# Linear attention and a gated two-layer network on one core: batch 0 loaded by casting transfers, more seven-product groups, chunk 4's sums by accumulating transfers, and normalising shared between VectorE, ScalarE and GpSimd

## The chip, the cores and the metric

The kernel runs on one core of one Trainium2 chip. The time is that of one execution on the device, in microseconds. Three runs of the kernel before took 278.95, 280.96 and 282.47 us; the median, 280.96, is what a changed kernel is compared with. One more execution was profiled: it took 283.07 us, of which the span from the first to the last instruction is 281.3 us.

## What is computed

```python
# q, k, v: (8, 8, 576, 64) float32;  theta = pi/2 * position/576
phi(x) = concat(relu(x)*cos(theta), relu(x)*sin(theta))     # 64 -> 128 features
kv  = einsum('bhsf,bhsd->bhfd', phi(k), v)
z   = sum over s of phi(k)
att = einsum('bhsf,bhfd->bhsd', phi(q), kv) / (einsum('bhsf,bhf->bhs', phi(q), z) + 1e-6)
x   = att, heads side by side: (4608, 512)
h   = x @ w_in                                              # (512, 2048)
out = (h * cos(h)) @ w_out                                  # (2048, 512), float32
```

The matrix products run in float16 with float32 sums.

## The kernel before

**Chunks.** Eight batches of 576 tokens are computed as nine chunks of 512 tokens: chunks 0 to 7 hold four tiles of 128 tokens of their batch (NT = 4), and chunk 8 holds the 64 tokens that each batch has left (R = 64, two batches to a tile). A batch lies on the partitions so that one tile index t is one column of `RAW`; tile 4 is the half-filled one, and its empty half is set to zero by a memset of `raw[nm][:, :, NT, :]`.

**Attention of a batch.** `load` (L264) brings q, k and v. For batches 1 to 7 these are transfers from POOL's queue that cast float32 to float16 on the way into `RAW`. Batch 0 is loaded by SP's queue as float32 into the buffers `raw0`, which borrow `gT` and `TT` (L206). `prep` (L282, L295 on ACT and L296 on DVE) applies relu and the cosine or sine of one tile and writes `KQ` (`kp` for k, `qp` for q). `cast_v` (L307, L308) copies v beside a column of ones into `V1`. `kv` (L319) sums the products over tiles in PSUM; the ones give z as the 65th column; `kvz` is its float16 copy. q is transposed by `q_pe` (L348 on PE, copies L352, L354) for batches 0 and 1 and by DMA (`q_dma`, L358) for the others. `num` (L380) multiplies the transposed q with kvz into a pair of PSUM banks; then `norm` takes the 65th columns plus 1e-6 (`den`, L412), the reciprocal (`rec`, L414) and the scaled rows (`x16`, L405), one DVE step of three instructions. `x_pe` (L437, copy L441) or `x_dma` (L447) transposes x16 into `xT`.

**Layers.** Layer 1 of chunks 0 and 1 runs as matmuls of 256 columns (L493); from chunk 2 on as plain matmuls of 512 columns (L525) or as groups of seven products (L620). Such a group replaces the 16 plain matmuls of four column blocks of w_in by 28 of 256 columns, after sums of w_in (`w_in_sums`, L556) and of xT (L577), and puts the products together again: three copies on ACT (L628), three sums on DVE (L632), one double cosine and product (L643, L649). `gate` (L467 on ACT, L469 on DVE) forms h*cos(h). `FAST` says how many of a chunk's groups run that way, the others being plain:

```python
todo = [g for g in range(NJT // 4) if g >= nf]
for g in range(NJT // 4):
    if g < nf:
        layer1_fast(c, g, X, xk)
    if g < len(todo):
        for j in [2 * todo[g] + i + JH * hf for i in range(2) for hf in range(2)]:
            layer1_plain(c, j, X, xk)
```

NJT is 16. Layer 2 of chunk 0 is plain (L722); from chunk 1 on it is seven products too (L796) over sums of g (L773, L826 on DVE). For the chunks in `ACC` two of these sums are accumulating transfers from POOL's queue (`add_dma`, L755).

**Order.** Every step is added to a list with its engine, the time that it is booked with, what it reads and what it writes. The text `ORDER` then says, as differences, in which order the steps are issued, and with a letter on which engine a step with a choice runs (D, A, P). The booked times and due times had a part in making that text and have none when the kernel is built. So each engine's instructions stand in one fixed order, and a step that waits holds up everything behind it on its engine. POOL's queue issues loads, w_in and w_out (L881, L887), the accumulating transfers and the stores of finished rows (L683).

**Start.** `warm` (L870) issues matmuls of 128x512 on a constant tile WZ (a part of S2, set by POOL's memset): 14 at the front, 16 ahead of kv, and 4, 3 and 2 between the first tiles (`FILL`). `weights` (L873) holds w_in's loads back until k of batch 0 has landed, by a copy of four elements.

Of the kernel before, what the change touches and what calls it, by code (L numbers as in the profile page):

```python
# [10 lines left out]
AF = mybir.ActivationFunctionType  # L11
ALU = mybir.AluOpType
# [4 lines left out]
ACC = (5, 6, 7)  # L17
POW = False
FAST = ((3, 2), (4, 2), (5, 2), (6, 4), (7, 4), (8, 4))
ORDER = (  # L20
    "1 6 1 -3 4 -6 7 1 1 1 1 1 18 1 -5 -7 -1 14 -5 -4 107D 1A -109 6 -25 17 -19 33 1D 8A 92 -136 "
    "38A 4D 93 -92D -3A 5D -31 27A -2D -24 22D 10A 3A -1D -3D 2A -23 -9 37D 2A -1D 2 -4A -1D 86 "
    "-115 35 1 -32 -9 42 -29 30 -26 27 77 -75 -1 -44 49 -1 3 -1 72 -76 9 -8 7 3 -1 67 -71 8 -7 8 "
    "1 59 -63 7 -6 65 9D -18 -49 63D 1D -67 62 -57 -4 3 71D -12 -55 -2 62D -61 4 -2 1 4 -2 57D "
    "-56 4 -2 58D -57 4 -2 54D -53 4 -2 50D -49 4 -2 50D -49 4 -2 175 -122D -4A -48 4 171 -173 "
    "63D -58 -2 -2 3 2 2 43A 4D -48 4 -2 38D -33 -4 2 55D -54 4 -2 53A -2D -50 36 -34 54 -14A 13D "
    "-52 4 47D -1D -21 6D 123 -104 -24 4 6D -3 18 -12D -2 -3 117 -93 -20 15 4 -5 101 -112 13 23 "
    "75 -110 17 -47 51 -1 -7 24 -68 45 8 14 710 -721 13 -8 90D -89 716 -721 -3 -5 100D -79 -20 8 "
    "86A 2A 2D 4D -93 88A -84 26 64A -81 73D -85 267 -272 95D 4D 117 -207 91D -69 -21 207 -182 "
    "82D -15 -70 188 -183 -19 15 75A 113 -120 -65 2 2 681 -617A -65 4 -2 73D -72 4 -2 66D -5A -60 "  # L30
    "4 -2 59 -27 24 -51 -36 91D -86 32 -5 61 -59 30 144A -205 32 60A 118A -175 58 1A -32 -26 61A "
    "-1 -54 -41 202A -4 -196 34 2 60 112A -11 -162 62 1 -61 -32 94 106A 6A -151 43 -1 -2 103A "
    "-200 101 -64 61 -63 172A -102 -104 38 159D -160 4 -2 311 -145A -165 63 -2 -59 2 158D -97 95A "
    "-153 55 244 -303 2 63 1 -3 4 -62 -51 119 101A -100 -4 232 -238 4 238 -299 62 -66 3 159 -157 "
    "161D 3A -67 -96 159A -209 140 78A -7 -99 31 -2 6 65D -95 27 -2 72 2A -68 59 12D -101 90 148D "
    "-136 135D -134A -76 4 -36 104 -62 -5 72A 135D -132 -73 -1 5 67 123 12D -134 -71 4 1 187 5A "
    "-196 10 -48 110 -230 163 2 190A -349 158 67 2 -64 -44 -2 230A -121 -61 63 -68 197A -235 42 "
    "65 -68 69 1 -65 5 61 119A -183 4 -5 66 117A -116 1 -115 53 -4 67 122A -184 69 109A -172 57 "
    "-67 5 314 -250 -118 117 -62 -53 239A 130 -252 -59 2 305 -123A -121 -67 7 309 -311 178 -182 7 "
    "-186 364A -238 54 187A -91 6 -4 2 88 -249 241 -79 91A -73 66 -82 -158 161 -40 38 4 -46 128D "  # L40
    "-83 -160 150 12 -4 5 -11 21 -8 -45 55 200A -133A -68 -172 375A -131D -245 2 244 2A -85 208A "
    "-188 -18 -159 237 -9 -231 163 2 -48 -115 2 240A -78 81 -83 84 113 -239 59 -176 -4 122 126 "
    "-77 203A -256 241 -187 -55 134 -245 363A -119 -65 188A -197 -10 -47 133 112A 149 -332 -61 53 "
    "9 71 -248 119 1 49 71 -59 68 -131 132 111A -240 49 8 66 -60 174D -107 -69 -59 60 196A -13D "
    "-114 2 -75 74 -60 -71 133 -83 -48 70 -9 71 -70 -61 1 61 193A -7D -185 -61 254 -21D -165 168A "
    "-173 -17 -44 60 315 -313 11 175A 126 -311 190A -186 -68 255A -184 87 -89 91 88A -86 -92 173 "
    "-168 171D -174 175 -83 -88 87 -157 67 185A -8 -85 -163 255A -98 7 76 -113 127 -75 63 -114 38 "
    "91 -252 162 216A -382 169 -5 -159 253 -91 90 -251 173 -50 130 -91 -161 123 256A -206 201A "
    "-223 -156 259 -90 -1 20 186 -204 90 -71 -59 131 -90 -172 180 202A -255 246 -110 2 -70 189A "
    "-210 200 -201 23 68 -5 -73 -11 -45 69 67 -134 49 197A -202 91 2 -1 -133 47 5 199D 1A -251 "  # L50
    "134 -79 -58 250A -112 -88 9 196A -250 50 -4 -50 63 76 -75 74 -133 238A 2D -179 -63 64 335 "
    "-351 8 12 69 -134 1 396 -142A -253 60 338 -334 186D -184 -5 -9 347 -334 4 -2 -5 200A -15 13A "
    "-188 91 -93 -2 183A -176 184D -188 181 -85 -91 89 83 -247 167 -95 96 92 -97 99D -90 235A "
    "-238 -163 247A -180 100 1 80 1D -254 75 99 -5 -37 45 -46 116 -241 398A -226 85 138A -226 -5 "
    "-169 254A -79 -169 257 -262 254 -72 -175 256 -130 50 -6 -176 183 -48 26 230 -261 6 256 -128 "
    "-131 -2 -130 177 -44 131 -88 2 5 213A -204 -13 5 -46 127 -72 -54 260A -214 83 -128 127 -69 "
    "197D -126 -75 5 -13 219A -210 75 1 1 -85 -51 66 -2 -4 213D -147 -121 132 -72 214A -226 214D "
    "-137 150A -228 16 190A -191 -59 130 -84 15 213A -207 -20 15 52 146D -196 -11 -52 256A 16 "
    "-210 2 -67 277D -199 -77 67 2 -66 68 196A -12D -177 -4 -4 198 -196 -78 269 7A 7 -268 270A "
    "-206 2 94 -90 190A -98 -6 -161 72 94 101 -105 98 -92 18 75 -130 42 -41 52 -10 -168 179 -22 "  # L60
    "-30 44 10 91 -421 420 -113 7 108 -87 -20 18 -183 168 3 96A -266 273 1 -106 -41 56 92 -114 12 "
    "12 -192 181 -12 114 -105 15 -192 283 1 -103 -47 144 -276 191 10 -68 -134 284 -84 73 -80 8 -4 "
    "-66 75 79 -87 -63 68 83 -109 -38 69 -14 13 -71 63 10 78 -102 -47 83 -84 82 -24 -9 -46 148 "
    "-68 -10 -69 1 69 -7 85 -67 69 -75 -20 16 5 10 -82 68 15 -23 20 -7 -75 83 -3 6 94 -179 180 "
    "-93 -1 -16 76 39 -105 103 -95 3 93 -182 69 21 -88 -1 86 -84 88 88 23 -18 16 -20 7 14 -113 "
    "101 17 -199 196 -15 -42 44 -182 199 -203 181 23 -61 46 16 -61 43 -182 201 -18 -38 -5 45 -334 "
    "337 14 1 -14 -193 146 44 4 17 -3 6 -2 -31 35 -1 -2 -63 67 16 49 -62 -29 -44 74 13 -10 -79 3 "
    "74 -23 40 -16 12 -35 -48 88 -87 83 -235 217 7 1 -17 -203 235 -14 16 -1 39 -127 90 -14 53 "
    "-132 136 -56 14 -90 77 -76 128 -74 75 -128 129 2 -39 -91 133 -45 4 43 -1 -41 -92 69 -9 87 "
    "-12 -65 75 -9 10 -145 77 59 -49 60 3 -13 14 -150 151 -64 53 -134 135 -64 -70 84 -90 7 120 14 "  # L70
    "-140 90 60 -15 -127 143 9 -8 -310 250 69 -34 -126 156 5 -4 -155 150 -8 14 7 -159 86 74 -13 9 "
    "16 -9 -2 -77 90 -12 -74 85 -44 35 1 10 -86 -2 43 39 -78 87 -183 95 90 -32 -56 47 40 -30 -56 "
    "89 -88 72 -71 75 11 -10 -75 61 26 -16 17 -26 -60 70 -71 91 -12 -77 86 4 -88 89 -4 -86 2 75 "
    "-71 -3 4 84 -87 88 5 -89 -3 82 11 -88 90 -1 -5 -85 86 6 -8 15 -12 7 6 -7 3 5 -6 2 8 -7 8 -4 "
    "5 1 1 -6 10 -9 8 -2 1 3 1 1 1 1 1 1 "
# [53 lines left out]
def kernel(  # L129
# [44 lines left out]
    def sb(name, shape, dt=F16):  # L174
# [31 lines left out]
    home0 = {"k": gT[0].rearrange("p h t j s -> p (h t j s)"),  # L206
             "q": gT[1].rearrange("p h t j s -> p (h t j s)"),
             "v": TT.rearrange("p n j s -> p (n j s)")}
    raw0 = {nm: heads_tokens(t.bitcast(F32)[:, 0:NR]) for nm, t in home0.items()}
# [20 lines left out]
    FILL = (4, 3, 2, 0)  # L230
# [3 lines left out]
    LATE_BY, LATE_W = (0.0, 0.8, 1.5, 1.0), 0.6  # L234
    LOAD_RATE = (355.0, 360.0)
    ORDER0, ORDER1 = "qkv", "kqv"
# [4 lines left out]
    B0, B1, B2, BP = 20.0, 56.0, 80.0, 27.0  # L241
# [12 lines left out]
    def either(due, cost, fn, rd, wr):  # L254

        lat = {"DVE": 0.13, "ACT": 0.15, "POOL": 0.15}
        pl.add([(e, cost[e], cost[e] + lat[e], fn[e]) for e in cost], 0, 0, due, None, rd, wr, port=True)
# [6 lines left out]
    def load(b, nm, due, hs=(slice(0, H),)):  # L264

        m, n = (raw0 if b == 0 else raw)[nm], b % 2
        q, eng = (nc.sync, "SP") if b == 0 else (nc.gpsimd, "POOL")
        for h in hs:
            five, four = tokens(src[nm][b][h])
            part = [(nm, hh, b == 0) for hh in range(H)[h]]  # L270

            def go5(h=h, five=five):
                q.dma_start(out=blocks(m, n)[:, h], in_=five)

            def go4(h=h, four=four):
                q.dma_start(out=blocks(m, 1 - n)[:, h, 0:NT, :], in_=four)
            nb = len(part) * R * D * 4 / 1e3
            occ = 0.65 if b == 0 else 0.9
            for go, k, x in ((go4, NT, 1 - n), (go5, NT + 1, n)):
                pl.add(eng, occ, 0, due, go, (), [(y, x) for y in part], dma=(nb * k, LOAD_RATE[b > 0]),  # L280
                       lane="first" if b == 0 else None, late=LATE_BY[min(b, 3)])
# [742 lines left out]
```

## Time and profile before

| | |
|---|---|
| median of three runs | 280.96 us (278.95 to 282.47) |
| profiled execution | 283.07 us, span 281.3 us |
| granted TensorE clock, mean | 0.994 |
| busy: PE, DVE, ACT, POOL | 269.9, 251.8, 210.5, 60.3 us |
| first layer-1 matmul | 21.56 us |
| layer 1 of chunk 0 in PE's order | 21.5 to 36.3 us |
| last matmul ends | about 277 us |
| instructions | 6759 |

PE is TensorE's matmuls and PEld its weight loads; DVE is VectorE, ACT ScalarE, POOL GpSimd, SP SyncE. Busy time is the time in which at least one instruction of an engine runs; matmuls overlap each other, so 256 columns take 0.109 us one behind the other (8 in 0.87 us in the chain of work) although one of them lasts 0.273. In a table of stretches the columns are busy time by engine, the granted clock of PE as a share of full speed, the busy share of the DMA engines, and GB/s moved. In a list of waits each line gives the engine and line that waits, what it waited for, the total, the number of times and the longest.

### The profile page before, as it was taken

What the parts mean: (1) busy time and instruction counts of PE and PEld (TensorE: products, weight loads), DVE (VectorE), ACT (ScalarE), POOL (GpSimd) and SP (SyncE); (2) the same over time, 40 slices, a digit from 0 to 9 for tenths busy, and PEclk for the clock granted to TensorE, in tenths of its full rate; (3) what the DMA queues carried; (4) which work ended last, traced back from release to release, by engine and by line L of the source; (5) the groups of instructions that cost most, each with busy time, mean ns of one, the idle gap of its engine ahead of it and who ended that gap; (6) DMA issues with size and microseconds to landing.
All of it is one profiled execution on the core that took longest, in us unless ns stands there. A gap on an engine that the chain in (4) does not pass through costs nothing.

```text
span 281.3 us, 6759 instructions
## 1 busy us (share of the span) xinstructions
PE 269.9 (96%) x2691; PEld 216.4 (77%) x2691; DVE 251.8 (90%) x484; ACT 210.5 (75%) x353; POOL 60.3 (21%) x98
## 2 busy tenths in 40 slices
PE   7799999998999799999999999999999999999994
PEld 2568876865956478787878787779988888888883
DVE  2879999897999799999999999999999999988952
ACT  2856876898899969889899987987576776657420
POOL 1472141410403300502323030002110220121300
PEclk9799999999999999999999999999999999999999
DMA  6999999999999999999999999486850434075124
GB/s 208 327 201 203 201 190 177 184 147 185 125 188 156 193 226 145 193 172 156 210 199 107 179 189 161 77 166 150 192 94 2 87 107 125 3 224 114 75 77 149
DMA packets 78463, 44.06 MB, mean 157 GB/s; under 512 B 46176, under 2 KB 75360, under 8 KB 78432
## 3 DMA queue, kind: packets, MB, share of 16 engines
q0 software_dynamic: 29856, 28.12, 57.5%
q1 hardware_dynamic: 47840, 14.95, 30.9%
q10 hardware_dynamic: 736, 0.57, 0.6%
q8 instruction: 21, 0.34, 0.5%
q14 instruction: 10, 0.08, 0.1%
HBM read 36.74 MB, written 9.44 MB: 164 GB/s over the span
## 4 chain that ended last, share of the span: by engine, by line
PE 82%; DMA 9%; DVE 5%; ACT 2%; issue 1%; SPq 0%; ACTq 0%
PE M L796 33%; PE M L620 14%; PE M L525 8%; DMA qT<-KQ 7%; PE TR L620 6%; PE M L493 4%; PE M L722 4%; PE ATT L380 3%; DVE gT L469 3%; PE ATT L319 3%; DMA gT<-in_q_dram 2%; PE TR L525 2%; PE M L348 2%; PE ATT L870 1%; ACT KQ L295 1%
## 5 line engine op out<-in xcount | busy, mean ns | idle before, releaser
L796 PEld LDWEIGHTS <-gT 128*128 128x128 f16 x560 | 54.1, 98 | 7.6
L295 ACT ACTIVATE KQ<-RAW,CS 128x512 f16<-128x512 f16 x86 | 59.1, 720 | 0.0
L796 PE MATMUL M<-w_out_sb,gT 128*128 128x256 f16 x448 | 56.2, 273 | 0.0
L467 ACT ACTIVATE ch<-M 128x512 f32<-128x512 f32 x75 | 44.1, 598 | 13.2 <-PE M L493 4.4
L469 DVE TENSOR_TENSOR gT<-M,ch 128x512 f16<-128x512 f32 x73 | 49.1, 684 | 3.1 <-ACT ch L467 2.3
L525 PE MATMUL M<-xT,w_in_sb 128*128 128x512 f16 x136 | 33.1, 379 | 0.0
L796 PE MATMUL M<-TT,S 128*128 128x256 f16 x256 | 32.0, 273 | 0.0
L807 ACT ACTIVATE ost<-M 128x512 f32<-128x512 f32 x32 | 19.1, 597 | 17.2 <-PE M L796 13.4
L493 PE MATMUL M<-xT,w_in_sb 128*128 128x256 f16 x256 | 29.7, 272 | 0.0
L683 POOL DMA_DIRECT2D out_dram<-ost x32 | 18.8, 611 | 47.2 <-DVE ost L811 25.7
L620 PEld LDWEIGHTS <-w_in_sb 128*128 128x128 f16 x264 | 25.4, 98 | 3.7
L796 PEld LDWEIGHTS <-S 128*128 128x128 f16 x256 | 24.6, 98 | 3.0
L628 ACT ACTIVATE Z<-M 128x512 f32<-128x512 f32 x31 | 18.2, 600 | 11.6 <-PE M L620 8.6
L493 PEld LDWEIGHTS <-w_in_sb 128*128 128x128 f16 x256 | 24.6, 98 | 3.0
L632 DVE TENSOR_TENSOR Z<-M,Z 128x512 f32<-128x512 f32 x38 | 25.4, 683 | 1.1 <-PE M L620 0.6
L525 PEld LDWEIGHTS <-w_in_sb 128*128 128x128 f16 x160 | 14.8, 98 | 13.1
L405 DVE TENSOR_TENSOR x<-ATT,rec 128x512 f16<-128x512 f32 x32 | 22.1, 691 | 1.1
L380 PEld LDWEIGHTS <-qT 128*128 128x128 f16 x320 | 15.7, 98 | 7.3 <-DMA qT<-KQ 3.7
L811 DVE TENSOR_TENSOR ost<-M,ost 128x512 f32<-128x512 f32 x24 | 16.4, 684 | 4.2 <-PE M L796 4.0
L380 PE MATMUL ATT<-kvz,qT 128*128 128x65 f16 x288 | 16.4, 194 | 3.0 <-DMA qT<-KQ 2.6
L296 DVE TENSOR_SCALAR KQ<-RAW,CS 128x512 f16<-128x512 f16 x54 | 18.3, 350 | 0.2 <-DMA RAW<-in_k_dram 0.2
L773 DVE TENSOR_TENSOR S<-gT 128x2048 f16<-128x2048 f16 x14 | 17.0, 1217 | 0.1
(133 smaller groups left out, 482.3 us busy)
## 6 DMA issues: line engine op xcount, KB each, us to landing
out_dram<-ost POOLq DMA_DIRECT2D x32, 256.0 KB, 4.7
RAW<-in_k_dram POOLq DMA_DIRECT2D x7, 320.0 KB, 5.3
RAW<-in_q_dram POOLq DMA_DIRECT2D x7, 320.0 KB, 7.6
w_in_sb<-in_moe_w_in_dram POOLq DMA_DIRECT2D x4, 512.0 KB, 9.8
w_out_sb<-in_moe_w_out_dram POOLq DMA_DIRECT2D x4, 512.0 KB, 12.1
RAW<-in_v_dram POOLq DMA_DIRECT2D x6, 320.0 KB, 7.4
RAW<-in_k_dram POOLq DMA_DIRECT2D x7, 256.0 KB, 6.4
RAW<-in_q_dram POOLq DMA_DIRECT2D x7, 256.0 KB, 6.7
```

Source lines behind the costliest of these rows:

```text
L295: fn = {"ACT": lambda: nc.scalar.activation(out=out_, in_=in_, func=AF.Relu, scale=sc), "DVE": lambda: nc.vector.tensor_scalar(out=out_, i ...
L380: nc.tensor.matmul(bank[hb][:, hh * D1:(hh + 1) * D1], lhsT=a[:, h, :], rhs=z[:, h, :], start=(i == 0), stop=(i == len(parts) - 1))
L405: nc.vector.tensor_tensor(out=split(x16[n][:, hs, :], k), in0=A[:, :, :, 0:D], in1=split(rec[n][:, hs], k).unsqueeze(3).broadcast_to((P, k ...
L467: act(0.5, due, lambda: nc.scalar.activation(out=ch[c], in_=bank, func=AF.Sin, bias=math.pi / 2.0, scale=1.0), [key], [("ch", c)])
L469: mul(due, 0.61, lambda q: q.tensor_tensor(out=dst, in0=bank.rearrange("p (j s) -> p j s", j=2), in1=ch[c].rearrange("p (j s) -> p j s", j ...
L493: nc.tensor.matmul(M1[m][:, jj * 2 * P:(jj + 1) * 2 * P], lhsT=w_in_sb[:, cc, j * P:(j + 1) * P], rhs=X[:, cc, ts], start=(cc == 0), stop= ...
L525: nc.tensor.matmul(M, lhsT=w_in_sb[:, cc, j * P:(j + 1) * P], rhs=X[:, cc, :], start=(cc == 0), stop=(cc == NCT - 1))
L620: nc.tensor.matmul(bank[0][:, j * TH:(j + 1) * TH], lhsT=a(cc, j), rhs=b[:, cc, :], start=(first and j == 0 and cc == 0), stop=(last and j ...
L632: dve(0.61, due + 0.3, lambda: nc.vector.tensor_tensor(out=dst, in0=bank[0], in1=dst, op=ALU.add), [bank[1], key], [key])
L683: pl.add(eng, 0.9 if eng == "POOL" else 0.65, 0, due, lambda: q.dma_start(out=dst, in_=src_), keys, [], dma=(nb, 355.0))
L796: nc.tensor.matmul(bank[0][:, tt * MH:(tt + 1) * MH], lhsT=a[:, j, tt * P:(tt + 1) * P], rhs=b[:, j, :], start=(first and (apart or tt == ...
L807: act(0.5, due, lambda: nc.scalar.activation(out=dst, in_=view(bank), func=AF.Copy), [bank[1]], dk)
```

## The change

- Batch 0 is loaded like the others: casting transfers on POOL's queue into `RAW`, k first, then v by halves of the heads, q by parts (tiles 0 and 1, tiles 2 to 4). Batch 1 uses the same form, and the buffers `raw0` are gone. The memsets of the empty halves stand in `setup`, once, on DVE, as do those of WZ, of V1's ones and of MINUS.
- k and v come before q in the first attention; 19 warming matmuls at the front and no others. w_in is no longer held back, and its first quarter comes in two pieces.
- Layer 1 of chunks 0 and 1 does its first quarter in pieces of 128 columns, each waiting for its own tile of xT.
- `FAST` asks for 26 groups in all, where it asked for 18.
- `ACC` holds chunk 4 too.
- The normalising is three steps with a choice of engine: the den sums on DVE or ACT, the reciprocal on DVE or, as a power of -1, on POOL, the scaling on DVE.
- `ORDER` is another text. In it, of 36 tiles, 28 have their den sums on ACT and 16 their reciprocal on POOL; 78 preps run on DVE and 82 on ACT, where it was 66 and 94.

```diff
-ACC = (5, 6, 7)
-POW = False
-FAST = ((3, 2), (4, 2), (5, 2), (6, 4), (7, 4), (8, 4))
+ACC = (4, 5, 6, 7)
+FAST = ((3, 3), (4, 4), (5, 4), (6, 5), (7, 5), (8, 5))
 ORDER = (
...
-    raw0 = {nm: heads_tokens(t.bitcast(F32)[:, 0:NR]) for nm, t in home0.items()}
...
-    FILL = (4, 3, 2, 0)
...
-    def load(b, nm, due, hs=(slice(0, H),)):
+    def load(b, nm, due, hs=slice(0, H), ts=range(NT + 1)):
 
-        m, n = (raw0 if b == 0 else raw)[nm], b % 2
-        q, eng = (nc.sync, "SP") if b == 0 else (nc.gpsimd, "POOL")
...
+        m, n = raw[nm], b % 2
+        five, four = tokens(src[nm][b])
+        heads = range(H)[hs]
+        for ap, k, x in ((four, NT, 1 - n), (five, NT + 1, n)):
+            t = slice(ts[0], min(ts[-1] + 1, k))
+            dst, ap = blocks(m, x)[:, hs, t, :], ap[:, hs, t, :]
+            wr = [((nm, h, i), x) for h in heads for i in sorted({min(j, 2) // 2 for j in ts})]
+            pl.add("POOL", 0.72, 0, due, lambda dst=dst, ap=ap: nc.gpsimd.dma_start(out=dst, in_=ap),
+                   (), wr, dma=(len(heads) * R * D * 4 / 1e3 * (t.stop - t.start), "ld"),
+                   late=LD_LATE[min(b, 2)])
...
-        def norm():
+        def sums():
             for A, (hs, k, ks) in zip(N, cut):
                 nc.vector.tensor_scalar_add(
                     out=split(den[n][:, hs], k), in0=A[:, :, :, D], scalar1=1e-6)
-            nc.vector.reciprocal(out=rec[n], in_=den[n])
-            scaled()
...
+        m = len(cut)
+        either(due, {"DVE": 0.1 + 0.06 * m, "ACT": 0.21 * m}, {"DVE": sums, "ACT": dens}, keys, [("den", n)], False)
+        either(due, {"DVE": 0.2, "POOL": 1.75}, {"DVE": lambda: nc.vector.reciprocal(out=rec[n], in_=den[n]), "POOL": recs},
+               [("den", n)], [("rec", n)], False)
+        dve(0.62 + 0.07 * m, due, scaled, keys + [("rec", n)], [("x16", n)])
         return n
...
+                        wk = [("w_in", quarter, jp)]
+                        if quarter == 0:
+                            for i in range(2):
+                                pe(2 * NCT, MMT, due, lambda i=i, mm=mm: mm(i * P, (i + 1) * P),
+                                   [xk[2 * hf + i]] + wk + [("M1", m)] * i, [("M1", m, 1)] if i else [("M1", m)])
+                        else:
+                            pe(2 * NCT, MMH, due, lambda mm=mm: mm(0, 2 * P), xk[2 * hf:2 * hf + 2] + wk,
+                               [("M1", m), ("M1", m, 1)])
...
     def setup():
-        nc.gpsimd.memset(S2[:, 0:2, :], 0.5)
+        nc.vector.memset(S2[:, 0:2, :], 0.5)
         nc.vector.memset(PIH, math.pi / 2.0)
+        for nm in "kvq":
+            nc.vector.memset(raw[nm][:, :, NT, :], 0.0)
+        nc.vector.memset(V1[:, :, :, D], 1.0)
+        nc.vector.memset(MINUS, -1.0)
...
     def weights():
-        def hold():
...
         for g in range(4):
-            fs = slice(g * Dff // 4, (g + 1) * Dff // 4)
...
+            for e in ((0,), (1,)) if g == 0 else ((0, 1),):
+                fs = slice(g * Dff // 4 + e[0] * Dff // 8, g * Dff // 4 + (e[-1] + 1) * Dff // 8)
...
     def first_attention():
...
-        warm(14, 6.5)
...
+        warm(19, 6.1)
+        load(0, "k", 0)
+        for h in HALVES:
+            load(0, "v", 1, h)
+        load(0, "q", 2, ts=(0, 1))
         weights()
...
+        load(0, "q", 3, ts=(2, 3, 4))
...
-            if FILL[t]:
-                warm(FILL[t], 0.2157 * FILL[t], M1[1],
-                     [(("ATT", "M2")[t % 2], 1)], [("M1", 1), ("fill", t)])
-            x_pe(0, t, t, *BANKS[3 - t % 2], "ACT", 8 + t, [("fill", t)])
```

`recs` is in the kernel before too, not called there: `nc.gpsimd.tensor_tensor(out=rec[n], in0=den[n], in1=MINUS, op=ALU.pow)`. On POOL a library reload stands in the built program ahead of the first of these.

## The prediction

> **What bounds the kernel now.** I read the page's busy shares first, then the busy time by stage (the windows), then the start in order of time, then the waits of PE.
>
> ```profile
> PE 269.9 (96%) x2691; PEld 216.4 (77%) x2691; DVE 251.8 (90%) x484; ACT 210.5 (75%) x353; POOL 60.3 (21%) x98
> ```
>
> PE is never far from full; the question is where the other 4% lies and how close DVE is.
>
> ```profile
> 0.00:8.20 8.20, 5.02 (x14) 1.73 (x14) 2.19 (x6) 2.19 (x4) 0.95 (x7) 1.00 0.71 230
> 9.50:11.20 1.70, 1.70 (x17) 1.70 (x18) 1.41 (x5) 0.96 (x2) 0.35 (x1) 0.50 1.08 357
> 21.50:36.30 14.80, 14.80 (x145) 13.27 (x143) 14.06 (x34) 11.29 (x20) 3.46 (x5) 1.00 1.30 203
> 41.10:77.40 36.30, 35.51 (x371) 26.06 (x369) 32.88 (x73) 29.77 (x52) 10.01 (x15) 1.00 1.24 164
> 77.40:100.00 22.60, 20.74 (x184) 12.68 (x181) 20.02 (x43) 19.70 (x34) 5.75 (x9) 1.00 1.24 181
> 100.00:200.00 100.00, 100.00 (x1033) 80.98 (x1031) 96.98 (x182) 87.31 (x147) 18.77 (x30) 1.00 1.01 168
> 260.80:275.70 14.90, 14.90 (x139) 13.36 (x137) 10.96 (x17) 4.39 (x7) 2.12 (x4) 1.00 0.18 71
> ```
>
> (Columns: stretch, length, busy time of PE, PEld, DVE, ACT, POOL, granted clock, DMA share, GB/s.) From 21.5 us PE is full but for 3.2 us in all (0.54 between 36.3 and 41.1, 0.79, 1.86). From 100 to 200, where the changed groups lie, PE has no hole and DVE has 3%: two engines bound it together. The start is 21.5 us in which PE does almost no layer work, and its last 5.6 us of the span are the tail.
>
> ```profile
> 8.28 0.90 PE L348 MATMUL TR<-IDENT,KQ 128*128 128x128 f16 x8 [1.94 <-ACT KQ L295]
> 9.50 1.89 PE L348 MATMUL M<-IDENT,KQ 128*128 128x128 f16 x16 [0.33 <-ACT KQ L295]
> 11.18 3.96 PE L870 MATMUL ATT<-S 128*128 128x512 f16 x16
> 14.98 0.61 PE L348 MATMUL M<-IDENT,KQ 128*128 128x128 f16 x8
> 15.43 1.37 PE L319 MATMUL M<-V,KQ 128*128 128x65 f16 x40
> 21.56 1.04 PE L493 MATMUL M<-xT,w_in_sb 128*128 128x256 f16 x8
> ```
>
> The filler of 16 (L870) runs while v is still landing (its casts start at 13.27); from there to the first layer-1 matmul is 8.3 us of chain.
>
> ```profile
> PE ATT L380 <- DMA qT<-KQ: 2.6, 2, 1.8
> ```
>
> This is the largest hole after the start.
>
> **The change, part by part.** All against the profiled execution: 283.07 us, of which 281.3 is the span. The three runs have a median of 280.96, so I scale the ratio of the spans to that.
>
> *Start.* Batch 0's loads move from SP to POOL as casting loads into RAW. SP's first issue is at 0.73; POOL's first now waits for DVE's memset of k's tail (S, then RAW; the RAW memset is 0.27 each), so about 1.5. In before, the first casting load was issued at 10.85 and its landing took 4.7; plain loads moved 357 to 365 GB/s, casting ones 203 to 206 (written bytes, half of those read), so q, k and v take 3.54 MB/0.365 = 9.7 us or 1.77/0.2 = 8.9 us: the stream itself gains under 1 us. With first bytes 2.1 us after issue (10.85 to the fall of the rate at 13) I get k and the first q part landed at about 8.3, v at 11.3, the rest of q at 12.9, against 13.3 for v before. Ten issues of 0.7 us are done by about 8.6, within that stream.
> Work behind it: 20 preps of float32 (DVE 0.48, ACT 0.71) become float16 ones (DVE 0.35, ACT 0.72); k and v come first, q after. From v: cast 0.35 and 0.28, kv 20 matmuls twice (0.6 each), kvz on ACT 0.39, num 0.29, den 0.16, a prep, reciprocal 0.20, scaling 0.69, then qT's copy 0.68 because in PE's order tile 2's num stands ahead of x_pe; x_pe 0.39, den on ACT 0.2, xT 0.60: about 6.1 with hops, so layer 1 at 17.4 against 21.56. It then takes 8 pieces of 128 columns (0.45 each) and 12 groups at the 0.87 of PE; the 14.8 us stage before becomes about 15.7, since DVE still has six multiplies, scalings and preps to catch up on. End of layer 1 of chunk 0: 33.1, was 36.3.
> That is with a warm clock. The three small fillers and the filler of 16 are gone; 19 matmuls at the front end at about 7.4 and then PE has only two transposes until kv. The clock row above reads 0.50 in 9.5 to 11.2 after 1.9 us without work, and it was 1.00 again from 13. The idle stretch now is longer, so I take kv, num and the first pieces at half clock: 3.4 us of PE work at double length, partly beside DVE, up to 1.6 us more (34.7). Gain between 3.2 and 1.6; I take 2.3, between them, as DVE paces part of that stretch. The Trainium skill ("TensorE: Matmul & The Clock Gate", Part 1) says that the clock is halved by default and is released only after some 3.4 us of sustained work; the trace agrees with its half clock. By that rule alone the gain is the 1.6 end and the total 0.7 us later; with no gating it is the 3.2 end.
>
> *POOL's queue at the start.* w_in now stands behind 1.77 MB, k and q of batch 1 between its pieces. Added up at 0.2 MB/us from 3.6: w_in's four quarters at about 15.5, 22, 25 and 28, v of batch 1 at 31, half of w_out at 37.5. Before they were (same rate from 13.4) 19 to 30, 33 and 38. PE wants them at 17.4, 22, 25.7, 29 and 38: hidden, by under 1 us. If POOL stalls at a load that waits for a prep (RAW is now shared by batches 0 and 1, as the separate buffers are gone), all behind it is late one for one.
>
> *Groups.* L620 has 504 matmuls before and 644 in the changed order: 18 groups become 23, not 26, since the loops run over NJT // 4 = 4 groups and the three 5s act as 4. Five more (one in chunk 3, two each in 4 and 5). PE: per group 28 x 0.109 - 16 x 0.216 = -0.41, so -2.0; the 128-column pieces add 128 x 0.056 - 64 x 0.109 = +0.2. DVE per group: three sums (0.684) and a double multiply (1.217) for two fewer single ones: +1.9. ACT: three copies (0.60), one double sine (1.06) for two fewer: +1.7. Five: DVE +9.5, ACT +8.3.
>
> *Sums of chunk 4 by transfers.* Two DVE additions (1.217 each) leave, -2.4; two POOL issues (0.88) come, landing in 4.7. Hidden as the three chunks that do so now are (PE has no hole in 160 to 260.8); uncovered, 4.7 - 1.2 = 3.5 each.
>
> *Normalising.* 28 of 36 den sums go to ACT (30 instructions), 16 reciprocals to POOL: DVE -30 x 0.157 - 16 x 0.203 = -8.0. ACT's is not in the trace: bounded by its 128x1 activation (0.20) and the 128x260 one (0.39), 6.0 to 11.7; nearest the first, 6.1. POOL's power on 128x8 is not there either: its memset of that very tile took 0.22, DVE's reciprocal 0.20; the kernel books 1.75. I take 1.75, the worse. Behind each, DVE's scaling waits in order and PE's next num or x_pe. By the order, DVE has 1.75 to 3.6 us of other work between den and scaling, PE 3.5 to 7.4 before the next step on those banks; the chain is 0.2 + 1.75 + 0.69 and hops. So hidden, with some 0.5 us to spare on DVE. A library reload stands before the first power. No row prices it; bounded by zero and a 512 KB landing (9.8), with 3.7 us of PE work over it: 0 to 6. I take 0, nearest the code packets of the page's queue list (21 of 16 KB, 0.5% of 16 engines' span: 1 us each). The Trainium skill ("GPSIMD Engine Reference", 2.1 Instruction dispatch) puts the first call of a freshly loaded kernel at about 6 us. By that the total would be 2.3 us more.
>
> *The rest* (DVE): 12 more preps there (+24 x 0.35 - 12 x 0.48 = +2.6), memsets and casts -1.8. Sum for DVE: 9.5 - 2.4 - 8.0 + 2.6 - 1.8 = 0. ACT: +8.3 + 6.1 - 12 x 0.72 = +6, off the bound overall but near 97% between 100 and 160.
>
> *Where DVE stands when the groups save PE 2 us.* Its sum stays and it was at 97%, so the stage cannot shrink by all of it: -1.8 if DVE gives up its idle time, +1 if it keeps it and ACT's load adds waits. I take -1.0. The 3.2 us of holes I leave as they are (0.7 to 8).
>
> Sum: 281.3 - 2.3 - 1.0 = 278.0, ratio 0.988, on the median 277.7.
>
> **Rivals.**
> 1. *DVE and ACT keep up and the holes close.* The new order has DVE free in the start, and the 2.6 us wait for qT is one of order. 281.3 - 3.2 - 1.8 - 2.5 = 273.8, on the median 273.5. Against it: DVE at 97%.
> 2. *DVE takes the whole gain.* The stretch 77 to 200 runs at DVE's pace with 3% idle, +3, and the start gives 2.3: about 281.5 us. For it: three engines all near 97% there.
> 3. *The power on POOL is longer than the work put before the scaling* (slower). Place: DVE's scaling, in order behind it everything of the co-bound engine. It decides from about 2.3 us a piece; at 3.2 it costs 16 x 0.9 = 14 less the 3.3 gained, about 291 us. For: no row shows a power; against: short POOL rows. The Trainium skill ("Advanced Engine Details and Errata", VectorE Performance Modes) says that POOL shares DVE's second port and the two block each other; no run here shows it. Each power would then also hold back a prep.
> 4. *The groups don't rise to 26*: certain by the counts above, and in the sum.
>
> **How the numbers follow.** Forecast 0.38 (275.5 to 280); rival 1 0.33 (271 to 275.3); rival 2 0.12 (280 to 285.5); rival 3 0.17 (over 286.5). About 2% is what a measurement of this kernel can tell from no change. Faster is rival 1, 0.33; slower rival 3, 0.17; the same 0.50. The range 271 to 286 leaves out rival 3 and a little below. The likeliest one's own is 275.5 to 280.
>
> **What would show it.** First layer-1 matmul between 17.4 and 19.1; granted clock 0.5 between 9 and 16; v landed near 11.3; casting loads at about 200 GB/s from 4 us on; 644 matmuls on the product line; DVE busy 249 to 254; PE holes after 35 us of 1 to 5 us; powers at 1.75 or less, with DVE not waiting for POOL. Wrong if layer 1 starts before 16 or after 20, if DVE's or PE's wait list names POOL, or if the reload shows as a hole of several us near 50.

## The result, and the profile after

The changed kernel is slower. Its four runs took 292.19, 294.40, 301.70 and 348.83 us beside 278.95 to 282.47 for the kernel before in the same session; the ratio is 1.045, 95% interval 1.032 to 1.059, where 0.988 was predicted. (The two longest ran over 1.5% above the fastest; such runs stay out of this ratio and of those below.) The profiled execution took 292.19 us with a span of 290.2 and a mean granted clock of 0.986.

The engines' busy times on the page of the profile after:

```profile
PE 268.4 (92%) x2795; PEld 222.1 (77%) x2795; DVE 250.1 (86%) x456; ACT 213.6 (74%) x378; POOL 99.4 (34%) x125
```

PE does slightly less than before (20 warming matmuls fewer) and DVE about the same, both in a longer span: most of the time is lost in idling. The same stretches as before, by engine:

```profile
0.00:8.20 8.20, 6.21 (x19) 2.27 (x19) 2.00 (x8) 1.49 (x2) 6.33 (x14) 1.00 0.78 92
21.50:36.30 14.80, 14.29 (x167) 12.73 (x165) 14.12 (x35) 10.92 (x21) 4.91 (x7) 1.00 1.36 200
41.10:77.40 36.30, 31.22 (x335) 22.33 (x334) 28.51 (x66) 25.51 (x48) 12.91 (x16) 0.95 1.23 169
77.40:100.00 22.60, 22.60 (x225) 15.77 (x224) 20.85 (x39) 20.51 (x38) 6.90 (x10) 1.00 1.31 169
100.00:200.00 100.00, 95.14 (x1023) 80.79 (x1022) 91.70 (x154) 89.12 (x158) 43.35 (x44) 1.00 1.09 164
```

In 41 to 77 us PE stands for 5 us, and in 100 to 200, which was full, for another 5. DVE is idle there too: 92 of 100 us where it had 97. No engine took the gain as a new bound; all of them wait. What PE waits for:

```profile
PE ATT L374 <- DMA qT<-KQ: 7.9, 6, 2.7
PE M L342 <- DVE KQ L289: 3.7, 2, 3.5
PE M L619 <- DVE gT L460: 1.2, 1, 1.2
```

The second line is the start. The first is the wait of the numerators (the products of `num`) for q's transposes (`q_dma`, L352 here), 2.6 us before. The longest pieces of it in the chain that ended last (start, length, what):

```profile
63.18 10.51 DMA qT<-KQ
```

```profile
187.13 6.14 DMA qT<-KQ
```

One transpose of q takes 10.5 us from issue to landing; the shortest take 3.0. Minimum, median and maximum over all 30, before:

```profile
DMA to landing us min/median/max: 3.0/4.3/11.7
```

and after:

```profile
DMA to landing us min/median/max: 3.0/6.1/11.5
```

The span can be split into the time to the first layer-1 matmul, PE's work from there, PE's holes (stretches without a matmul) from there and what follows the last matmul (all from the matmul records):

| | first layer-1 | work | holes | tail | span |
|---|---|---|---|---|---|
| before | 21.56 | 252.7 | 3.2 | 3.9 | 281.3 |
| after | 19.64 | 255.2 | 11.5 | 3.9 | 290.2 |
| difference | -1.9 | +2.5 | +8.3 | 0 | +8.9 |

Of the +2.5 of work 1.7 is one stretch of 3.41 us at half clock, from 73.67, right behind the longest hole. So the holes and what follows from them cost 10.0 us and other work 0.8, against 1.9 gained at the start.

What stands around the longest hole on POOL's queue:

```profile
59.58 1.83 POOL L395 TENSOR_TENSOR rec<-den,MINUS 128x8 f32<-128x8 f32 x1 [4.79 <-ACT den L391]
61.36 1.41 POOL L272 DMA_DIRECT2D RAW<-in_q_dram  x2
62.76 1.38 POOL L272 DMA_DIRECT2D RAW<-in_v_dram  x2
```

A power (the reciprocal on POOL) waits 4.79 us for the sums of a numerator, and four casting loads behind it leave together; the transpose issued at 63.18 lands at 73.69, with the v load issued at 63.43 (73.67).

### The profile page after: what moved, and what is told of

Same layout as the page of the kernel before. It is cut to its first block, busy times and chain, and to the rows that moved or that the text cites. A ratio compares the mean times of both kernels' runs of the same rounds, so it can differ in the third digit from the quotient of the medians.

```text
span 290.2 us, 7034 instructions
## 1 busy us (share of the span) xinstructions
PE 268.4 (92%) x2795; PEld 222.1 (77%) x2795; DVE 250.1 (86%) x456; ACT 213.6 (74%) x378; POOL 99.4 (34%) x125
## 4 chain that ended last, share of the span: by engine, by line
PE 54%; DMA 17%; DVE 16%; ACT 4%; issue 4%; POOL 3%; SPq 0%; DVEq 0%; POOLq 0%; ACTq 0%
PE M L795 23%; PE M L619 11%; DMA qT<-KQ 9%; PE M L483 6%; DVE gT L460 5%; DMA xT<-x 5%; PE TR L619 4%; PE M L722 3%; PE M L521 3%; DMA RAW<-in_q_dram 2%; DVE KQ L289 2%; DMA RAW<-in_k_dram 2%; PE ATT L374 2%; DVE Z L631 2%; POOL RAW L272 2%
## 5 line engine op out<-in xcount | busy, mean ns | idle before, releaser
L460 DVE TENSOR_TENSOR gT<-M,ch 128x512 f16<-128x512 f32 x61 | 40.7, 684 | 5.2 <-ACT ch L458 4.9
L395 POOL TENSOR_TENSOR rec<-den,MINUS 128x8 f32<-128x8 f32 x16 | 29.8, 1862 | 43.8 <-ACT den L391 43.7
L458 ACT ACTIVATE ch<-M 128x512 f32<-128x512 f32 x63 | 36.7, 598 | 10.6 <-PE M L483 5.0
L631 DVE TENSOR_TENSOR Z<-M,Z 128x512 f32<-128x512 f32 x53 | 35.7, 684 | 3.4 <-PE M L619 2.2
L619 PEld LDWEIGHTS <-w_in_sb 128*128 128x128 f16 x324 | 31.0, 98 | 6.4 <-issue 2.0
L289 DVE TENSOR_SCALAR KQ<-RAW,CS 128x512 f16<-128x512 f16 x78 | 26.2, 363 | 10.9 <-DMA RAW<-in_k_dram 5.9
L483 PE MATMUL M<-xT,w_in_sb 128*128 128x256 f16 (+1 forms) x320 | 31.8, 256 | 0.3 <-DVE gT L460 0.3
L627 ACT ACTIVATE Z<-M 128x512 f32<-128x512 f32 x43 | 25.0, 598 | 9.5 <-PE M L619 9.4
L483 PEld LDWEIGHTS <-w_in_sb 128*128 128x128 f16 x320 | 26.4, 100 | 4.0 <-issue 0.5
L806 ACT ACTIVATE ost<-M 128x512 f32<-128x512 f32 x32 | 19.1, 599 | 11.6 <-PE M L795 7.9
L374 PEld LDWEIGHTS <-qT 128*128 128x128 f16 x320 | 16.1, 99 | 15.0 <-DMA qT<-KQ 10.2
L642 ACT ACTIVATE ch<-Z 128x1024 f32<-128x1024 f32 x21 | 22.2, 1059 | 4.0 <-DVE Z L631 3.6
L399 DVE TENSOR_TENSOR x<-ATT,rec 128x512 f16<-128x512 f32 x32 | 21.9, 686 | 3.2 <-DMA xT<-x 1.1
L648 DVE TENSOR_TENSOR gT<-Z,ch 128x1024 f16<-128x1024 f32 x18 | 21.9, 1217 | 0.0
## 6 DMA issues: line engine op xcount, KB each, us to landing
w_out_sb<-in_moe_w_out_dram POOLq DMA_DIRECT2D x4, 512.0 KB, 10.2
```

What stands on the lines that cost most here:

```text
L289: "DVE": lambda: nc.vector.tensor_scalar(out=out_, in0=in_, scalar1=0.0, scalar2=sc, op0=ALU.max, op1=ALU.mult)}
L374: nc.tensor.matmul(bank[hb][:, hh * D1:(hh + 1) * D1], lhsT=a[:, h, :], rhs=z[:, h, :], start=(i == 0), stop=(i == len(parts) - 1))
L395: nc.gpsimd.tensor_tensor(out=rec[n], in0=den[n], in1=MINUS, op=ALU.pow)
L458: act(0.5, due, lambda: nc.scalar.activation(out=ch[c], in_=bank, func=AF.Sin, bias=math.pi / 2.0, scale=1.0), [key, *rda], [("ch", c)])
L460: mul(due, 0.61, lambda q: q.tensor_tensor(out=dst, in0=bank.rearrange("p (j s) -> p j s", j=2), in1=ch[c].rearrange("p (j s) -> p j s", j ...
L483: nc.tensor.matmul(M1[m][:, jj * 2 * P + lo:jj * 2 * P + hi], lhsT=w_in_sb[:, cc, j * P:(j + 1) * P], rhs=X[:, cc, h0 + lo:h0 + hi], start ...
```

## The experiments

Two theories to begin with. A: loads stand behind powers on POOL's queue, leave late and bunched, and delay the transposes. B: the new order puts four numerators only 4.0 to 4.8 us of PE work (by the booked times) behind their transposes, where the shortest such distance before was 5.2; it would fail with any queue. C, beside them: chunk 4's accumulating transfers delay transposes. Times are medians; ratios are to the kernel before, with 95% intervals.

**Reciprocals back on DVE.**

```diff
-  POOL: 16 powers at their places in ORDER
+  DVE:  16 reciprocals, each right ahead of its scaling
```

> The changed kernel with the 16 reciprocals on DVE, each right ahead of its scaling; every other place in the order is unchanged. Theory A (POOL's queue: loads stand behind powers that wait for a numerator, so they leave late and in bunches, and q's transposes land with them): the numerators' waits for q's transposes fall from 7.9 us to 3 or less, and the time from 292.2 to about 286 although DVE has 3.2 us more (16 x 0.2). Theory B (the order gives the transposes 3.6 to 4.8 us of PE work where they need 5 to 6): those waits stay at 6 to 8 and the time at 291 to 295. The rival of the prediction (the power itself is too long): DVE's and PE's waits behind scalings go, 2 to 4 us.

Measured: 313.0 us, ratio 1.106 (1.093 to 1.118), by the ratios 17 us worse than the changed kernel. Neither theory had that. POOL's queue now runs ahead:

```profile
58.16 1.36 POOL L272 DMA_DIRECT2D RAW<-in_q_dram  x2 [2.69 <-ACT KQ L288]
59.50 1.38 POOL L272 DMA_DIRECT2D RAW<-in_v_dram  x2
```

and the same transpose that took 5.6 us in the changed kernel (issued at 58.25, three microseconds before the loads) is now issued 0.4 us before them:

```profile
57.80 11.42 DMA qT<-KQ
```

**Loads ahead of the powers, powers kept.**

```diff
-  POOL: power, load q, load q, load v, load v
+  POOL: load q, load q, load v, load v, power        (13 loads in all)
```

> The changed kernel with 13 loads on POOL's queue put ahead of the power that they stood behind. Theory A: waits for q's transposes 4 us or less, the hole of 2.66 us at 73.7 gone, 286 to 288 us. Theory B: only the 2.66 us change, the other four waits of 0.65 to 2.0 stay, 290 to 293 us.

Measured: 309.0 us, 1.097 (1.086 to 1.107). Theory A falls: loads that leave earlier make it worse, and by the same event. (Here powers stand behind loads, and DVE waits 3.6 us for four of them; that can't be the cause in the run before, which has no powers.)

```profile
58.40 1.36 POOL L272 DMA_DIRECT2D RAW<-in_q_dram  x2 [2.70 <-ACT KQ L288]
59.74 1.38 POOL L272 DMA_DIRECT2D RAW<-in_v_dram  x2
```

```profile
58.05 11.62 DMA qT<-KQ
```

In three kernels one transpose, issued at 57.8 to 58.25, lands after 11.4, 11.6 or 5.6 us, as the loads leave 0.35, 0.35 or 3.1 us behind it. That gave theory K: a transpose of q lands with the casting loads that leave up to some tenths of a microsecond after it, and the order's distances hold for one arrangement of loads only. K is a rule of thumb: in the changed kernel the transpose issued at 212.32 takes 8.28 us with no load of q, k or v near it, among a store and an accumulating transfer.

**Numerators later.**

```diff
-  PE: ... num(t) some 4 to 8 us of work behind q_dma(t) ...
+  PE: ... num(t) some 7 to 12 us behind, what hangs on it moved along ...   (7 tiles)
```

> The changed kernel with seven numerators (and what hangs on each) put 4 to 23 places later in the order, so that 7 to 11 us of PE work instead of 3.6 to 7.9 lie between the issue of q's transpose and its numerator. Theory B: waits for q's transposes under 2 us, no stretch at half clock after 73 us, 282 to 285 us. Theory A: the powers come later too and hold the loads longer; the waits move but keep 5 us or more, 289 us or more.

Measured: 291.2 us, 1.035 (1.027 to 1.043). Waits for transposes are gone and the half clock too, yet the holes are 11.4 us, where the changed kernel has 11.5: what followed the numerators had no room either.

```profile
PE TR L428 <- DVE x L399: 1.9, 1, 1.9
PE ATT L312 <- DVE x L399: 1.9, 1, 1.9
PE ATT L374 <- DVE x L399: 1.7, 2, 1.4
DVE x L399 <- POOL rec L395: 5.1, 3, 2.6
```

PE waits for scalings (L399), and those in part for powers: 5.1 us, where DVE waits 0.4 for one power in the changed kernel. So B named a real wait, but not the one thing to mend: a numerator's chain (sum, power, scaling, next user of the bank) needs its own distance.

**Chunk 4's sums on DVE again.**

```diff
-ACC = (4, 5, 6, 7)
+ACC = (5, 6, 7)
```

> The changed kernel with chunk 4's two sums on DVE again, at the places of the two transfers. Theory C (chunk 4's transfers collide with q's transposes near 187 us): the 2.0 us wait at 193 us goes, transposes issued from 176 to 192 land in 3 to 5 us instead of 4 to 8, and the time falls by 1 to 2 us in spite of 2.4 us more on DVE. Theories A and B: the wait stays at 1.5 or more, time the same to 2 us longer.

Measured: 289.8 to 298.8 us, median 294.8, no interval: unclear in time. Its trace is clear: the 2.0 us wait at 193 is gone, the transpose that took 6.1 us there takes 3.2, and DVE's 2.4 us more made no new hole of that size. C holds for that wait.

**Powers to nobody.**

```diff
-            nc.gpsimd.tensor_tensor(out=rec[n], in0=den[n], in1=MINUS, op=ALU.pow)
+            nc.gpsimd.tensor_tensor(out=SCR[n], in0=den[n], in1=MINUS, op=ALU.pow)
...
+                nc.vector.reciprocal(out=rec[n], in_=den[n])   # ahead of the scaling
```

> The changed kernel with DVE computing the 16 reciprocals just ahead of the scalings, as in the run before, while POOL still does the 16 powers at their places, with the same waits, into a tile that nobody reads: POOL's loads leave when they did in the changed kernel. Theory K (collisions: what the run with reciprocals on DVE lost came from the loads leaving earlier and landing on top of q's transposes): back from 309 to within 3 us of the changed kernel's 292. Theory P (DVE's reciprocal as such, or the length of the power): stays over 300 us, or, if the power's length was a cost of the changed kernel, falls under 289.

Measured: 293.5 us, 1.048 (1.043 to 1.053). With POOL's queue as it was, DVE's reciprocals cost nothing and taking the power out of the chain saves nothing: the 17 us of the first run came from when the loads left. K holds for it, and the prediction's rival of a power that is too long falls.

**Two thirds of the later loads left out, in both kernels.**

```diff
+        if b > 1 and nm != "q":
+            issue = lambda **kw: None        # keys and values of batches 2 to 7
```

> The changed kernel without the loads of k and v from batch 2 on (leaves out: the keys and values of batches 2 to 7 are those of batches 0 and 1); nothing else moves. Theory K: with two thirds of the casting traffic gone q's transposes land in 3 to 4.5 us (median 6.1 in the changed kernel), their waits fall from 7.9 us to under 2, and the time to 281 to 284. Theory O (the order is too tight for its chains, whatever the traffic): holes after the start stay over 8 us and the time over 288.

> The kernel before without the loads of k and v from batch 2 on (leaves out the same as the changed kernel's run). Theory K: only the 2.6 us of waits for q's transposes to be had, so 278 to 280 us, and the changed kernel without these loads comes within 4 us of it. Theory O: 278 to 280 as well, but the changed kernel stays 8 us or more behind.

Measured: changed kernel 284.1 us, 1.013 (1.008 to 1.018); kernel before 279.5, 0.997 (0.994 to 1.000). The waits for transposes and their landings in the changed kernel:

```profile
PE ATT L378 <- DMA qT<-KQ: 2.2, 2, 1.8
```

```profile
DMA to landing us min/median/max: 3.0/3.5/12.1
```

and the landings in the kernel before:

```profile
DMA to landing us min/median/max: 3.0/3.3/7.6
```

By the ratios (1.045 less 1.013) this traffic costs the changed kernel 9 us and the kernel before 1. What stays, 4.6 us, goes with 8.0 us of holes in that profile: 3.5 of them behind DVE's gates, 2.2 still behind transposes, DVE not full (17.6 of 20 us in 100 to 120). That it is the order's other chains is the likely reading, not a shown one.

**The same with reciprocals on DVE.**

```diff
+   both edits: no loads of k and v from batch 2 on; 16 reciprocals on DVE
```

> The changed kernel without the loads of k and v from batch 2 on (leaves out the same as before) and with the 16 reciprocals on DVE. It tells what is left of the changed kernel's loss when nothing lands on top of the transposes. If the rest (284.1 against 279.5 us) is POOL's loads standing behind powers: 280 to 281.5. If it is the order itself (chains between engines without room): 283 to 286, DVE's 3 us more included.

Measured: 290.3 us, 1.035 (1.028 to 1.043), outside both expectations. The loads of q alone, once they leave earlier, bring the median landing, 3.5 us in the run above, close to the 6.1 of full traffic:

```profile
PE ATT L378 <- DMA qT<-KQ: 4.7, 3, 2.2
```

```profile
DMA to landing us min/median/max: 3.0/5.6/11.5
```

So when the loads leave matters beside how many they are. How much is less sure: of the 4.7 us between the spans of the two profiles 2.2 are holes, and 2.3 are a later first layer-1 matmul (22.02 against 19.69), in a start that the two kernels share.

**Chunk 4's transfers alone, in the old order.**

```diff
-ACC = (5, 6, 7)
+ACC = (4, 5, 6, 7)                  # in the kernel before
```

> The kernel before with chunk 4's two sums by transfers at the places where DVE did them, nothing else changed. The prediction had this hidden (0, with -2.4 us on DVE); theory C has the transfers collide with transposes and stores: 1 to 3 us longer than before, with new waits for q's transposes or for the sums between 150 and 190 us.

Measured: 288.1 us, 1.029 (1.024 to 1.034). That is 7.8 us more than before. A sum of 1.2 us on DVE became a transfer that took 7.55 us among loads and stores, and DVE, in order, stood behind it; PE followed, with 6.8 us at half clock:

```profile
165.96 7.55 DMA gT<-gT
```

```profile
DVE S L773 <- DMA gT<-gT: 7.3, 1, 7.3
PE M L796 <- DVE S L773: 4.8, 1, 4.8
```

**The casting start alone, in the old order.**

```diff
-        q, eng = (nc.sync, "SP") if b == 0 else (nc.gpsimd, "POOL")
+        q, eng = nc.gpsimd, "POOL"
-    raw0 = {nm: heads_tokens(t.bitcast(F32)[:, 0:NR]) for nm, t in home0.items()}
+    raw0 = {nm: heads_tokens(t[:, 0:NR]) for nm, t in home0.items()}
```

> The kernel before with batch 0's eight loads as casting loads on POOL's queue into float16 (same places in the order, same tiles), nothing else changed. If the start's gain is the loads' alone: first layer-1 matmul at 20 us or earlier instead of 21.56 and 279 us or less. If the gain needs the new order behind it, or is given back where the casting stream still runs (to 59 us): first layer-1 matmul within 0.7 us of 21.56 or waits later on, 280 to 283 us.

Measured: 1.004 (0.999 to 1.010), first layer-1 matmul at 20.56. No gain; its ten runs spread from 279.9 to 289.5 us (median 284.2). The profiles also show how much that mark moves by itself: with the old start it stood at 20.13, 20.42, 21.38 and 21.56, with the changed kernel's at 19.64 to 20.60 in nine, at 21.02 and at 22.02. With the old start the two late ones are the two that show half clock (3.41 us from about 8.3); the changed start, without the small fillers, shows it every time, for 3.4 us or, in the runs with reciprocals on DVE (20.30 and 22.02), for 6.8.

**The changed kernel's steps in a new order.** Two orders with other places for half of PE's steps, made with the landing times of these runs, one with chunk 4's sums on DVE.

```diff
-  ORDER of the changed kernel
+  same steps, 225 of PE's 453 elsewhere   (245 with ACC = (5, 6, 7))
```

> The changed kernel with the same steps in another order (225 of PE's 453 steps, and as many of DVE's share, stand elsewhere; 9 steps change between DVE, ACT and POOL), made so that q's transposes have the landing times that the runs showed. If landing times and room in the order are the whole cause: holes after the start 4 to 6 us instead of 11.6, waits for q's transposes under 2, 282 to 286 us. If something else in the new parts costs (the groups, the powers): holes stay over 9, 288 or more.

> The same kind of new order, with chunk 4's sums on DVE. If chunk 4's transfers were a burden beyond their place in the order: 1 to 3 us below the run with the transfers. If not: the same to 1.5 us above it, for DVE's 2.4 us more.

Measured: 285.6 to 299.2 and 284.0 to 294.7 us over four runs each, no interval. Inconclusive: the best runs are where room in the order would put them, the others not; both profiles (299.2 and 294.7 us) are of such others, with single transposes of up to 15.6 us. That an order fitted to landing times pays for their spread would fit this, and is not shown.

**Loads held until a transpose has landed.**

```diff
+            if b > 2 and last:
+                nc.gpsimd.tensor_copy(out=HOLD, in_=last[-1][:, 0, 0:1])
             nc.gpsimd.dma_start(**kw)
```

> The changed kernel where POOL, ahead of each load of batches 3 to 7, reads one column of the tile that the last transpose of q ahead of it in the order writes, so the load leaves only when that transpose has landed. Theory K (a transpose lands with the casting loads that leave up to half a microsecond after it): median landing of q's transposes from 6.1 to 4.5 us or less, the wait of 2.66 us at 73.7 gone. The loads then leave 3 to 8 us later, so k, v and q themselves come late: between 286 and 296 us. If the transposes stay at 6 us, other traffic (stores, sums, x's transposes) is what slows them, and theory K falls for the loads.

Measured: 309.8 us, 1.092 (1.083 to 1.101). The 2.66 us wait is gone and the median fell from 6.1 to 5.2, so loads that follow do delay a transpose. It did not fall to the 4.5 expected, and the time is far above the 296: other traffic may have its share, and the loads are now late for everything else.

```profile
DMA to landing us min/median/max: 3.0/5.2/9.2
```

```profile
PE ATT L383 <- DVE x L408: 4.9, 1, 4.9
PE ATT L383 <- DMA qT<-KQ: 3.9, 3, 2.1
PE M L628 <- DVE gT L469: 3.4, 1, 3.4
```

By the ratios, earlier loads cost 14 to 17 us against the changed kernel and later ones 13: of the arrangements tried, its own suits the order best.

**The added groups without their load on DVE and ACT.**

```diff
+        light = (c, g) in ((3, 2), (4, 2), (4, 3), (5, 2), (5, 3))
-            act(0.5, due + 0.3, lambda: nc.scalar.activation(
+            act(0.5, due + 0.3, lambda: light or nc.scalar.activation(
-            dve(0.61, due + 0.3, lambda: nc.vector.tensor_tensor(
+            dve(0.61, due + 0.3, lambda: light or nc.vector.tensor_tensor(
```

> The changed kernel in which the five added groups leave out their three copies on ACT and three sums on DVE (leaves out those partial sums: 15 x 0.68 on DVE, 15 x 0.60 on ACT, about what the five groups add), PE's products and the order as they are. If the groups' load on DVE and ACT makes the holes behind the gates: 4 us or more faster than the changed kernel, 288 or less, holes of 100 to 200 us nearly gone. If the transposes are the cause: 1 to 2 us at most.

> The same, and without the loads of k and v from batch 2 on. It splits what was left without that traffic (284.1 against 279.5 us for the kernel before): near 280 if the groups' load on DVE and ACT is the rest, 283 to 284 if it is the chains of the order.

Measured: 295.1 us, 1.048 (1.041 to 1.056), with all loads; 283.9, 1.012 (1.004 to 1.019), without those of k and v. With the traffic the groups' load is not the cause:

```profile
PE ATT L374 <- DMA qT<-KQ: 10.5, 6, 3.0
PE M L620 <- DVE gT L460: 0.4, 1, 0.4
```

The wait for a gate shrinks from 1.2 to 0.4 us, and the waits for transposes grow from 7.9 to 10.5. Without the traffic the profile has 5.0 us of holes instead of 8.0, but the medians are the same (283.9 and 284.1), so whether the groups hold part of the last 4.6 us stays open.

**One numerator later, in the kernel before.**

```diff
-  PE: num 10.4 us of work behind its transpose (the 1.82 us wait at 97.7 us)
+  PE: num 13.9 us behind
```

> The kernel before with one numerator (the one behind the 1.82 us wait at 97.7 us) 19 places later in the order, its transpose given 13.9 instead of 10.4 us of PE work. If the wait is one of order alone: 1 to 2 us faster than before, 278.5 to 279.5. If what hangs on it (its scaling, the next product of k and v on the same bank) waits instead: no change, as the run with seven numerators later showed for the changed kernel.

Measured: 281.0 us, 1.002 (0.999 to 1.006), twelve runs: no change. The wait goes and the next product on that bank waits 1.3 us for the scaling. No version tried here beats the kernel before.

## Why the prediction was wrong

**The step that failed** is "the 3.2 us of holes I leave as they are (0.7 to 8)". They became 11.5, and a half-clock stretch behind the longest added 1.7 to PE's work. The prediction had weighed queues and waits one by one against the work that covered them. By leaving the holes alone it took, without saying so, that q's transposes land as in the trace of before (median 4.3 us) and that the new order leaves them as much room. Neither held: 21 of 30 transposes now took over 5 us, where 11 had, and four numerators stand closer behind theirs than any did before. Without the loads of k and v from batch 2 on, 9 of the 13 us of loss are gone; the last 4.6 stay open. Between the predicted span of 278.0 and the measured 290.2 lie 12.2 us: 8.3 of holes, 3.5 of work (+2.5 for -1.0, with the 1.7 of half clock in it) and 0.4 of start. The tail, read as 5.6 us, is 3.9 behind the last matmul, and stayed.

**Start.** 19.64 was measured, 17.4 to 19.1 predicted; layer 1 of chunk 0 ended at 35.35 (22.85 and 12.50 in the line below), predicted 33.1 to 34.7, before 36.3. The clock was at half from 12.23 to 15.65, as foreseen (9 to 16). The term that was off is v's landing, 12.6 for 11.3: the first load left at 2.00 for 1.5, and the stream ran at 189 to 195 GB/s from 5 us on, for 200 from 4. From there to layer 1 it took 7.0 us, where 6.1 with up to 1.6 for the clock were foreseen.

```profile
12.81 2.45 PE L312 MATMUL M<-V,KQ 128*128 128x65 f16 x40
19.64 1.06 PE L483 MATMUL M<-xT,w_in_sb 128*128 128x128 f16 x16
22.85 12.50 PE L483 MATMUL M<-xT,w_in_sb 128*128 128x128 f16 x128 [0.33 <-DVE gT L460]
```

The gain of 1.9 holds against the one profile shown: old starts were seen from 20.13, changed ones up to 22.02. The mechanism was right, the size was taken against a late start, one with half clock in it.

**POOL's queue at the start** held: w_in's pieces landed at 15.8 to 30.2, two us later than worked out, and PE waited for none.

**Groups.** 644 matmuls on the product line, so 23 groups, as counted. Counted from one matmul's start to the next one's, PE's products rose by 15.9 us and the plain line fell by 17.3: -1.4, not -2.0. In the run without the k and v loads, which has no half clock behind the start, it is -1.7, and the small pieces cost 0.1; but PE's transposes, numerators and layer 2 took 1.7 more there, so that its work, 252.8 against 252.7, shows nothing of the 1.8 that the groups were to save.

**Chunk 4's transfers** were booked as hidden, uncovered 3.5 us each. In the old order they cost 7.8 us (288.1 less 280.3), as much as two uncovered ones, because DVE waits in order behind a transfer that leaves among loads. In the new order the sums are hidden (DVE waits for none), and the price appears on the transposes: the 2.0 us at 193, which went when the sums were on DVE.

**DVE's and ACT's sums** came near: DVE 250.1 us (no change from 251.8 predicted), ACT 3 us more (6 predicted).

**Normalising** was right in its terms and wrong in what it hid. The powers took 1.69 us in the median (1.75 booked), DVE waited 0.4 us for one of them in all (of the prediction's signs of being wrong the only one that showed), and there was no reload to see. That the loads stand behind them was not weighed at all, and it is what the order turned out to rest on.

```profile
L395 POOL TENSOR_TENSOR rec<-den,MINUS x16: 1637/1685/2440, 59.6 to 230.2; 128x8 f32<-128x8 f32 x16
L395 POOLq MODIFY_POOL_CONFIG  x2: 44/44/44, 54.8 to 54.8; - x2
```

The first power began when its sum was there; in the run with loads first it began 0.1 us after MODIFY_POOL_CONFIG and took 1.72. The Trainium skill ("GPSIMD Engine Reference", 2.1 Instruction dispatch) puts a load of about 6 us ahead of the first call; the traces do not show it here. Nor did a power slow DVE: its 128x512 gates took 0.682 us beside one and 0.683 elsewhere, its 128x2048 additions 1.217 both ways, its preps 0.341 and 0.346 in the median.

**The rivals.** 1, the holes close: the opposite came. 2, DVE takes the gain: DVE had 86% of the span and waits itself. 3, slower by the power's length: about the right time (291) by luck, for a wrong reason, as the powers to nobody showed. 4, 23 groups: right. The case that came, late transposes under a tighter order, was none of them; its nearest mark was the row of q's waits in the profile before, read as one of order alone.

## What to carry to other kernels

A transfer's latency in a profile belongs to what else leaves around it: before a queue's order changes, look in the trace at which transfers leave within a microsecond of the ones that an engine waits for, and book those by their worst landing, not the median. A delay that looks harmful, here loads behind a waiting power, may be what keeps two transfers apart; take it away alone, and see, before building on it. In a program ordered by hand to a few microseconds, a part is worth what the order has room for: of the two parts tried alone here the casting start gained nothing, and chunk 4's transfers, taken as free, cost 7.8 us. The groups and the shared normalising were not tried alone.

## What was not expected of the hardware

Casting loads and transposes of q slow each other strongly: a transpose of 128 x 1024 float16 lands in 3.0 to 3.3 us by itself and in 10.5 to 12.6 beside four loads of 1152 KB together, which took 10.2 to 14.5 us with loads first, where they took 4.8 to 10.2 in the changed kernel. The Trainium skill ("DMA: Bandwidth & Descriptors", Queues, rings and completion order) says that each DMA engine takes turns between the queues it has work for, a packet at a time; a transpose that lands with loads issued after it agrees with that. The prediction did not weigh it. The packet records of the changed kernel show how the two kinds share: from 69 to 73 us the transposes' queue moved 972 packets and the loads' queue 932, nearly one for one, 60 GB/s beside 125, where the transposes' queue alone moved 206 (79 to 80 us) and the loads alone 202 (74 to 75 us). With the reciprocals on DVE it was 880 packets each in the same stretch.

PE's clock fell to half for 3.41 us after a hole of only 2.66: in the 3.41 us ahead of it PE had worked about 0.8. The Trainium skill ("TensorE: Matmul & The Clock Gate", Part 1) gives windows of that length; the trace agrees, and adds that a window need not be empty.
